# A gated MLP in seven products: a staged tile's place, and when four raw weight rows are loaded

## The chip, the cores and the metric

The kernel runs on one core of one Trainium2 chip. The metric is device time in microseconds (us) of one execution; the times shown are medians of a few runs. The profile is of one execution, taken by the hardware profiler.

## What is computed

```
g = x @ w_gate          # x: 2048 x 1024, w_gate and w_up: 1024 x 3584, bfloat16
u = x @ w_up
h = gelu(g) * u         # tanh approximation
out = h @ w_down        # w_down: 3584 x 1024
```

## The kernel before

The 2048 rows are worked on in two passes (`ip`) of two blocks (`c`) of 512 rows. A pass has a gate/up stage and a down stage. Both are written as Strassen-like schemes with seven block products instead of eight: sums and differences of blocks of the weights (`s1` to `s4`, `sums_s`, line 170), of x (`t1` to `t4`, line 155) and of the down weights are formed beside the products, and TensorE (PE) multiplies them as 128x128 weights against 128x512 blocks into eight PSUM banks.

**Gate/up stage.** It goes through 14 units of 256 columns, `u` = 0 to 13. Units 4 to 11 go in pairs (`pair0` in the first pass, line 357, `pair1` in the second), the others one by one (`unit`, line 238). For each unit the raw weights are loaded by two DMAs of 512 KB into a tile "w" (`load_w`, line 138), GpSimd (POOL) forms their sums (`pool`, line 110), ScalarE (ACT) copies banks to SBUF (`snap`, line 123) and applies the gelu (line 198), VectorE (DVE) adds and multiplies (`dve`, line 107; `times`, line 205, writes gelu(g)*u to h).

**Tiles and slots.** Three pools matter. `kpool` has 36 slots of 2 KB a partition, taken in turn by `slot` (line 97): gelu results, bank copies, raw rows and many others. A new tile takes a slot when its last tile's readers are done. `wpool` has three large buffers named "w": unit weights, later four raw rows of w_down together, and loads of made sums. `mpool` has two, named "m", for the sums of w_down.

**h that has no room yet.** While x's sums (`forms`) hold the place of the late part of h (`hL`), units 9 to 11 of the first pass put nine tiles elsewhere (`away`): eight in one "w" buffer (`staged`, line 296), the ninth in a slot of `kpool` named hx (line 865). `bring_home` (line 346) copies both to hL by DMA near the end of the last pair.

**The sums of w_down.** The down stage needs, for j = 0 to 13, three differences of blocks of w_down's rows. They are made once, in the first pass, and stored in DRAM (`td`, `store_made`, line 534). `fetch_wd` (line 501) loads the two raw rows of a j, 256 KB each: for j up to 9 into two slots, for 10 and 11, and for 12 and 13, four rows into one "w" buffer. Sums 0 to 9 are made by ScalarE and VectorE through a bank (`keep_part`, line 512, two of them in each pair, 8 in unit 12, 9 in unit 13), sums 10 to 13 by GpSimd alone (`keep_whole`, line 526, three subtractions each): 10 and 11 in `prepare` of unit 12, 12 and 13 in that of unit 13 (line 899). `making` (line 799) gives [8] for unit 12 and [9, 10, 11, 12, 13] for unit 13.

**Down stage** (`down`, line 630). Its steps are counted; an agenda says what is issued at a step (`at`, line 605), and `more` (line 964) adds stores and the next pass's loads. Steps 0 to 27 multiply h with raw tiles of w_down of 256 KB (`fetch12`, line 587, fourteen of them, numbered 0 to 13 here, each for two steps or eight matmuls; "tiles of the down stage"); the first four are fetched in unit 13 (line 935). Meanwhile `make12` (line 559) forms two sums of h for each j on VectorE, 28 operations whose operands lie in SBUF, and `load12` (line 541) loads the made sums back, at first two j's in a 1 MB DMA into a "w" buffer. From step 28 on come the products with those sums.

**What sets the order.** VectorE, GpSimd, PE and the DMA queue run in the order of the code (`ORDER`, line 69); ScalarE too in the gate/up stages. All DMAs are issued by SyncE (SP) on one queue, in order: an issue that waits holds up all behind it. In the built program an issue also waits until the DMA eight before it has landed.

Of the kernel before, what the change touches and what calls it, by code (L numbers as in the profile page):

```python
# [10 lines left out]
def kernel(  # L11
# [26 lines left out]
    P = nc.NUM_PARTITIONS  # L38
# [186 lines left out]
    def add(ps, other):  # L225
        g = new(dve, ps[0], other[0], ADD, "sum", dtype=f32)
        dve(ps[1], ps[1], other[1], ADD)
        return g, ps[1]

    def finish_raw(u, c, p1):  # L230
        g, up = add(c, p1)
        times(2 * u, 0, gelu(g), up)

    def into(ps, src):
# [3 lines left out]
    def unit(u, banks, s, t, late, after_p5, aside, keep, ahead_of_p4, behind_p4, turned):  # L238
        GU = range(2)
        e, c, d = banks  # L240
        aside(-2)
        g, up = late() if late else (None, None)
        aside(-1)
        for i in GU:
            product(e[i], s["s2"][i], t["t2"], False)
        aside(0)
        keep(0, c)
        u2 = [snap(e[i], "u2") for i in GU]
        if late:
            g = gelu(g)  # L250
        c11 = g, up
        keep(1, c)
        keep(2, c)
        c = d
        for i in GU:
            product(c[i], s["s1"][i], t["t1"], True)
        p5 = [snap(c[i], "p5") for i in GU]
        after_p5()
        for i in GU:
            product(e[i], s["s3"][i], t["t3"], False)  # L260
        if turned and u % 2:
            turned(banks[1])
        elif turned:
            g, up = add(e, p5)
            times(2 * u + 1, 1, gelu(g), up)
            turned(banks[1])
        else:
            g, up = new(dve, e[0], p5[0], ADD, "sum", dtype=f32), banks[1][not late]
            dve(up, e[1], p5[1], ADD)
        if late:  # L270
            times(2 * u, 0, *c11)
        for i in GU:
            product(c[i], s["s4"][i], t["tb"], False)
        if not turned:
            times(2 * u + 1, 1, gelu(g), up)
        aside(1)
        g, up = add(c, u2)
        times(2 * u, 1, gelu(g), up)
        if turned and u % 2:
            g, up = add(e, p5)  # L280
            times(2 * u + 1, 1, gelu(g), up)
        ahead_of_p4()
        for i in GU:
            product(e[i], s["sa"][i], t["t4"], False)
        behind_p4()
        if turned:
            dve(e[1], e[1], p5[1], SUB)
        times(2 * u + 1, 0, gelu(e[0]), e[1])
# [3 lines left out]
    T1, T2, T3, T4, TB = [[forms[:, 2 * n + i] for i in range(2)] for n in range(5)]  # L292
    pd = dpool.tile([P, LAST - FIRST + 1, 2, N], f32, name="pd")
    st8 = []

    def staged(n, c):
        if not st8:
# [513 lines left out]

    def raw_of(u, e):
        p1 = raw_products(e, K, xT, W(u))
        return lambda: finish_raw(u, K, p1)

    def upgraded(u):
        return FIRST <= u <= LAST
# [29 lines left out]
    for ip in range(NPASS):  # L847
        with tc.manual_schedule(engines={ENG.Activation}):
            if ip == 0:
                ws = {1: w, 2: ahead}  # L850
                late = lambda: add(cc, nxt["p1"])
            else:
                raw_of(0, F)()
                raw_of(1, C)()
            for u in range(1 if ip == 0 else 0, NU):
                if upgraded(u):
                    if u % 2:
                        continue
                    if u == FIRST:
                        S = {u: s, u + 1: sums_s(W(u + 1), pool)}  # L860
                    if (ip, u) == (0, FIRST):
                        for n in range(4):
                            for c in range(2):
                                away[NH + n, c] = lambda n=n, c=c: staged(n, c)
                        away[NH + 4, 0] = lambda: slot([P, N], bf16, "hx")

                    def hooks(what, n):
                        if what == "w":
                            W(n)
                            if ip == 0 and n - 3 in JS:  # L870
                                fetch_wd(JS[n - 3][1:])
                            if ip and n <= LAST:
                                fetch_p5(n)
                        if what == "home" and n == LAST:
                            bring_home()
                        if what == "pd":
                            k = 0 if n % 2 else KH
                            nc.sync.dma_start(
                                out=pd[:, n - FIRST].rearrange("p i n -> p (i n)"),
                                in_=flat(xT[1][:, k : k + KH]),  # L880
                            )
                        if what == "made":
                            store_made(n)
                        if what == "fetch":
                            fetch_wd(JS.get(n + 2, [8, 10, 11])[: 1 if n + 2 in JS else 3])

                    roles = F, C, K, E
                    if ip == 0:
                        F, C, K, E = pair0(u, roles, S, t, JS[u], hooks)
                    else:  # L890
                        F, C, K, E = pair1(u, roles, S, t, hooks)
                    if u + 1 == LAST:
                        s = make_s(None, pool, S[u + 2])
                        nxt["s"] = S[u + 3]
                    continue
                js = making(u) if ip == 0 else []
                first = (ip, u) == (0, 1)

                def prepare():
                    if first:  # L900
                        pool_behind(t["t4"][-1])
                    if u + 1 < NU:
                        nxt["s"] = make_s(W(u + 1), pool, nxt.get("s"))
                    if ip == 0:
                        if js:
                            store_made(js[0])
                        if u == NU - 2:
                            for j in making(u + 1)[1:3]:
                                keep_whole(j)
                        if u == NU - 1:  # L910
                            for j in js[3:]:
                                keep_whole(j)
                        if u == FIRST - 2:
                            fetch_wd(JS[FIRST][:1])

                def keep(part, ps):
                    if js:
                        keep_part(js[0], part, ps[part // 2])
                    if ip == 0 and u in (2, 3):
                        lo_part(u - 2, part, ps)  # L920

                def aside(part):
                    if first and part < 0:
                        rest_of_0(part + 2)
                    if part == 0 and u + 2 < NU:
                        W(u + 2)
                        if ip and upgraded(u + 2):
                            fetch_p5(u + 2)
                        if (ip, u) == (0, 1):
                            load_lo()  # L930
                    if part == 0 and (ip, u) == (0, NU - 2):
                        fetch_wd([9, 12, 13])
                    if part == 0 and (ip, u) == (0, NU - 1):
                        for n in range(4):
                            fetch12(n)
                            ahead12.add(n)
                        for j in js[1:3]:
                            store_made(j)
                    if part == 0 and "t4" not in t:
                        t.make("t4")  # L940

                def ahead_of_p4():
                    if u % 2 and u + 1 < NU:
                        raw_of(u + 1, F)()
                        nxt["c11"] = raw_of(u + 2, C)

                def behind_p4():
                    if "c11" in nxt:
                        nxt.pop("c11")()

                if u % 2 and not first:
                    E, K, C = C, E, K
                banks = (E, K, C) if u % 2 else (F, K, E)
                turned = (lambda c: lo_part(u - 2, 3, c)) if ip == 0 and u in (2, 3) else None
                unit(
                    u, banks, s, t, late if first else None, prepare, aside, keep,
                    ahead_of_p4, behind_p4, turned,
                )
                s = nxt.pop("s", None)
# [4 lines left out]
        def more(step):  # L964
            if last:
                return
            if step in (0, 2):
                store_made({0: NJ - 2, 2: NJ - 1}[step])
            if step == 0:
                xT[:] = new_x()  # L970
            if step >= 24 and step % 2 == 0 and step // 2 - 12 < len(moves):
# [43 lines left out]
```

## Time and profile before

| | us |
|---|---|
| median of 3 runs (540.96 to 541.69) | 541.0 |
| the profiled execution | 542.6 |
| its span, first to last instruction | 540.8 |
| PE busy | 531.4 |
| VectorE, ScalarE, GpSimd busy | 363.4, 276.2, 269.0 |
| DMA: hardware queue q1 | 103.44 MB, 64.4% of 16 engines |
| HBM read, written | 78.64 MB, 19.40 MB |
| first pass: gate/up ends, first 28 steps of down end | 200.1, 224.8 |
| second pass: gate/up begins, the down stage's products with w,q begin | 288.7, 473.8 |

The granted PE clock is 1.00 in the whole profile. In a timeline line come the start and the length in us, engine, source line, operation, out<-in by the program's names, the shape, how often it is repeated, and in brackets the idle time ahead of it and what ended that. Busy time of PE is counted with overlap: each matmul is some 0.38 us long and starts 0.22 us after the one before, so gaps are read from the starts. A line number is often that of a helper: L108 is any VectorE operation, L111 any of GpSimd's, L132 any matmul; the names of the tiles tell which.

### The profile page before, as it was taken

The page shows a single profiled execution, that of the slowest core. Times are in us where ns is not written, and L with a number is a line of the kernel's source. Part 1 is how long each engine was busy: PE and PEld are TensorE (multiplying, and loading weights), DVE is VectorE, ACT ScalarE, POOL GpSimd, SP SyncE. Part 2 cuts the span into 40 slices and gives each one's busy share as a digit, 9 for nine tenths or more (in the row PEclk, how much of TensorE's full clock was granted, in tenths as well). Part 3 has the DMA queues.
Part 4 walks back from the last instruction along what each step waited for, and adds up shares of the span by engine and source line. Part 5 has one row for each costly group of instructions (what it writes and reads, how often), then busy time and mean ns, then how long its engine had stood idle before and what let it go on. Part 6 is the DMA issues. An engine that isn't in the chain of part 4 may idle for free.

```text
span 540.8 us, 7482 instructions
## 1 busy us (share of the span) xinstructions
PE 531.4 (98%) x2372; PEld 377.5 (70%) x2393; DVE 363.4 (67%) x564; ACT 276.2 (51%) x497; POOL 269.0 (50%) x253
## 2 busy tenths in 40 slices
PE   9999999999999999999999999999999999999997
PEld 5568686868686664588886867668667685488886
DVE  2987867777775879658587455576675749775830
ACT  3557676868683741015345645656666551104351
POOL 1079986979798480000006949793979620000000
PEclk9999999999999999999999999999999999999999
DMA  9795063946769799989995443343561239655571
GB/s 245 174 232 167 1 175 117 279 150 196 233 196 320 252 388 365 337 253 216 259 322 151 122 137 99 115 120 113 160 189 28 57 102 383 235 175 161 170 240 53
DMA packets 115527, 103.91 MB, mean 192 GB/s; under 512 B 21792, under 2 KB 97696, under 8 KB 115360
## 3 DMA queue, kind: packets, MB, share of 16 engines
q1 hardware_dynamic: 115488, 103.44, 64.4%
q8 instruction: 19, 0.31, 0.3%
q14 instruction: 20, 0.16, 0.1%
HBM read 78.64 MB, written 19.40 MB: 181 GB/s over the span
## 4 chain that ended last, share of the span: by engine, by line
PE 89%; DMA 4%; DVE 3%; ACT 2%; issue 1%; SPq 0%; DVEq 0%; ACTq 0%
PE bank L132 89%; DMA raw<-in_w_down_dram 2%; DMA hL<-hx 1%; DVE bank L108 1%; DMA xn<-in_x_dram 1%; ACT g L200 1%; DVE hT L108 1%; DVE forms L108 0%; DVE sum L108 0%; DVE m L108 0%; DVE hL L108 0%; ACT bank L519 0%; SPq L707 0%; ACT forms L840 0%; ACT u L125 0%
## 5 line engine op out<-in xcount | busy, mean ns | idle before, releaser
L111 POOL TENSOR_TENSOR s<-w 128x512 fp32r<-128x512 bf16 x102 | 120.2, 1194 | 138.7 <-PE bank L132 107.5
L132 PE MATMUL bank<-t,s 128*128 128x512 f32 x552 | 132.1, 392 | 1.0 <-DVE m L108 0.7
L132 PEld LDWEIGHTS bank<-t,s 128*128 128x128 f32 x552 | 103.5, 188 | 23.9 <-DVE m L108 1.1
L132 PE MATMUL bank<-xT,w 128*128 128x512 bf16 (+1 forms) x489 | 108.0, 376 | 2.3 <-DMA raw<-in_w_down_dram 0.9
L132 PEld LDWEIGHTS <-w 128*128 128x128 bf16 x504 | 47.8, 98 | 60.0 <-issue 6.6
L200 ACT ACTIVATE g<-sum 128x512 f32<-128x512 f32 x81 | 51.5, 635 | 65.9 <-DVE sum L108 60.0
L125 ACT COPY p<-bank 128x512 f32<-128x512 f32 x102 | 57.7, 590 | 50.0 <-PE bank L132 50.0
L108 DVE TENSOR_TENSOR sum<-bank,p 128x512 f32<-128x512 f32 x54 | 37.1, 687 | 38.1 <-PE bank L132 37.0
L108 DVE TENSOR_TENSOR hT<-g,bank 128x512 bf16<-128x512 f32 x72 | 49.1, 687 | 16.3 <-ACT g L200 9.9
L111 POOL TENSOR_TENSOR s<-w,s 128x512 fp32r<-128x512 bf16 x50 | 57.9, 1174 | 0.9 <-PE bank L132 0.6
L111 POOL TENSOR_TENSOR s<-s,w 128x512 fp32r<-128x512 f32 x50 | 57.4, 1164 | 0.4
L132 PE MATMUL bank<-tb,s 128*128 128x512 f32 x216 | 54.4, 394 | 1.2 <-ACT p L125 1.2
L132 PE MATMUL bank<-t,sa 128*128 128x512 f32 x216 | 55.1, 397 | 0.0
L120 ACT CAST tb<-raw 128x512 fp32r<-128x512 bf16 x28 | 17.5, 630 | 73.4 <-PE bank L132 30.3
L108 DVE TENSOR_TENSOR bank<-bank,p 128x512 f32<-128x512 f32 x72 | 49.8, 695 | 7.4 <-PE bank L132 7.4
L132 PE MATMUL bank<-q 128*128 128x512 f32 x208 | 51.7, 389 | 0.0
L132 PEld LDWEIGHTS bank<-tb,s 128*128 128x128 f32 x216 | 40.4, 188 | 10.5 <-POOL w L111 1.5
L132 PEld LDWEIGHTS bank<-t,sa 128*128 128x128 f32 x216 | 40.6, 188 | 9.1
L132 PEld LDWEIGHTS bank<-q 128*128 128x128 f32 x208 | 39.0, 188 | 8.1
L125 ACT COPY u<-bank 128x512 f32<-128x512 f32 x56 | 32.1, 594 | 15.7 <-PE bank L132 15.7
L132 PE MATMUL bank<-raw,hT 128*128 128x512 bf16 x140 | 31.2, 379 | 0.2
L108 DVE TENSOR_TENSOR q<-raw 128x512 fp32r<-128x512 bf16 x28 | 19.2, 687 | 17.9 <-DMA raw<-in_w_down_dram 10.3
(80 smaller groups left out, 636.1 us busy)
## 6 DMA issues: line engine op xcount, KB each, us to landing
raw<-in_w_down_dram SPq DMA_DIRECT2D x72, 256.0 KB, 5.1
w<-in_w_gate_dram SPq DMA_DIRECT2D x27, 512.0 KB, 4.7
w<-in_w_up_dram SPq DMA_DIRECT2D x27, 512.0 KB, 5.9
q<-td SPq DMA_DIRECT2D x52, 256.0 KB, 4.4
td<-m SPq DMA_DIRECT2D x12, 768.0 KB, 5.3
w<-td SPq DMA_DIRECT2D x6, 1024.0 KB, 9.8
pd<-xT SPq DMA_DIRECT2D x8, 512.0 KB, 4.6
out_dram<-st SPq DMA_DIRECT2D x32, 128.0 KB, 1.9
```

The costliest lines, as they stand in the source:

```text
L108: nc.vector.tensor_tensor(out=out, in0=a, in1=b, op=op)
L111: nc.gpsimd.tensor_tensor(out=out, in0=a, in1=b, op=op)
L120: nc.scalar.copy(out=t, in_=src)
L125: nc.scalar.copy(out=t, in_=ps)
L132: nc.tensor.matmul(ps, lhsT=lhs, rhs=rhs, start=start, stop=stop, skip_group_check=True)
L200: nc.scalar.activation(g, src, ACT.Gelu_apprx_tanh)
```

## The change

Three edits, all in the first pass.

1. hx gets a tile of its own in the pool of x, and takes no slot.
2. The raw rows of j = 10 and 11 were loaded with those of 8 at the end of the last pair, and 12 and 13 with 9 in unit 12. Now 8 alone is loaded at the end of the last pair, 9, 10 and 11 in unit 12, and 12 and 13 in unit 13, after the first four tiles of the down stage and after the store of sum 10. The stores of sums 11, 12 and 13 are issued at steps 0, 3 and 6 of the down stage; before, 11 was stored in unit 13, and 12 and 13 at steps 0 and 2.
3. In unit 3, `times(2 * u + 1, 1, g, up)` moves on VectorE from ahead of `raw_of(u + 1, F)()` to between its adds and its own `times`. On ScalarE the gelu stays where it was.

The orders on PE, ScalarE and GpSimd are the same before and after; on VectorE one instruction moves by two places, on SP the loads and stores named above move.

```diff
-    def finish_raw(u, c, p1):
+    def finish_raw(u, c, p1, mid):
         g, up = add(c, p1)
+        if mid:
+            mid()
         times(2 * u, 0, gelu(g), up)
...
+        mid = None
         if turned and u % 2:
             g, up = add(e, p5)
-            times(2 * u + 1, 1, gelu(g), up)
-        ahead_of_p4()
+            g = gelu(g)
+            mid = lambda: times(2 * u + 1, 1, g, up)
+        ahead_of_p4(mid)
...
+    hx = xpool.tile([P, N], bf16, name="hx")
...
-                        away[NH + 4, 0] = lambda: slot([P, N], bf16, "hx")
+                        away[NH + 4, 0] = lambda: hx
...
                         if what == "fetch":
-                            fetch_wd(JS.get(n + 2, [8, 10, 11])[: 1 if n + 2 in JS else 3])
+                            fetch_wd(JS.get(n + 2, making(LAST + 1))[:1])
...
                     if part == 0 and (ip, u) == (0, NU - 2):
-                        fetch_wd([9, 12, 13])
+                        fetch_wd([9, 10, 11])
                     if part == 0 and (ip, u) == (0, NU - 1):
                         for n in range(4):
                             fetch12(n)
                             ahead12.add(n)
-                        for j in js[1:3]:
-                            store_made(j)
+                        store_made(js[1])
+                        fetch_wd(js[3:])
...
-                def ahead_of_p4():
+                def ahead_of_p4(mid):
                     if u % 2 and u + 1 < NU:
-                        raw_of(u + 1, F)()
+                        raw_of(u + 1, F)(mid)
...
-            if step in (0, 2):
-                store_made({0: NJ - 2, 2: NJ - 1}[step])
+            if step in (0, 3, 6):
+                store_made(NJ - 3 + step // 3)
```

More of the change, by code (lines that the diff above doesn't have):

```diff
@@ L813, in raw_of @@
         p1 = raw_products(e, K, xT, W(u))
-        return lambda: finish_raw(u, K, p1)
+        return lambda mid=None: finish_raw(u, K, p1, mid)
     def upgraded(u):
```

## The prediction

> **What bounds the kernel now.** I read the page first, then TensorE's timeline by stages, then what released the first instruction after each of its gaps, and at last the DMA queue. The profiled execution took 542.6 us, its span 540.8; the median of the runs shown is 541.0, so I work with differences and add them to the median.
>
> Page, parts 1 and 4: TensorE is busy for 98% of the span and holds 89% of the chain.
>
> ```profile
> PE 531.4 (98%) x2372; PEld 377.5 (70%) x2393; DVE 363.4 (67%) x564; ACT 276.2 (51%) x497; POOL 269.0 (50%) x253
> ...
> PE 89%; DMA 4%; DVE 3%; ACT 2%; issue 1%; SPq 0%; DVEq 0%; ACTq 0%
> ```
>
> A change off TensorE is worth only what it does to TensorE's gaps. Between 63 us and the end of the first pass's gate/up work they stand here (timeline of TensorE):
>
> ```profile
> 176.00 3.02 PE L132 MATMUL bank<-xT,w 128*128 128x512 bf16 x12 [0.93 <-DMA raw<-in_w_down_dram]
> ...
> 181.59 2.10 PE L132 MATMUL bank<-t,s 128*128 128x512 f32 x8 [0.71 <-DVE m L108]
> 183.94 2.06 PE L132 MATMUL bank<-t,s 128*128 128x512 f32 x8 [0.25 <-ACT u L125]
> ...
> 196.43 2.07 PE L132 MATMUL bank<-tb,s 128*128 128x512 f32 x8 [1.16 <-ACT p L125]
> ...
> 221.26 1.89 PE L132 MATMUL bank<-raw,hL 128*128 128x512 bf16 x7 [0.21 <-DMA raw<-in_w_down_dram]
> 223.31 1.89 PE L132 MATMUL bank<-raw,hL 128*128 128x512 bf16 x8 [0.16 <-DMA raw<-in_w_down_dram]
> ```
>
> The brackets count from the modelled end of the matmul before. From start to start, less the usual 0.22 us of one matmul, the six cost 1.1, 0.9, 0.4, 1.3, 0.4 and 0.3 us. The first is put down to a DMA that had long landed; ScalarE's timeline and the DMA issues' tell what it was:
>
> ```profile
> 174.59 0.63 ACT L200 ACTIVATE g<-sum 128x512 f32<-128x512 f32 x1 [4.63 <-DMA hL<-hx]
> ```
>
> ```profile
> 167.70 0.60 SPq L350 DMA_DIRECT2D hL<-hx  x1
> ```
>
> That gelu's result takes the slot in which hx lies, so it waits for hx's copy, which lands at 174.51.
>
> **hx gets its own place.** The gelu's sum ends at 171.28, so it starts 3.2 us earlier. Down the chain (times, kept sums of 7: lines 200, 108, 519) TensorE itself becomes the limit: ScalarE's second p1 copy must wait for four matmuls that end at 176.0 and can start 2.7 us earlier, not 3.2. The last kept sum of pair 7 (180.84 + 0.69 = 181.53) then ends near 178.75, 2.8 earlier; TensorE reaches the bank at 179.4, so the 0.9 gap goes too. I call the end of this sum X. The store of sum 7, pair 9, four big rows, the store of sum 8 and the first four tiles of the down stage hang on X in both orders in the same sequence, so the 1.3 gap at 196.43 (a kept sum waits for the store of sum 8) stays, X + 14.9. TensorE enters the down stage 2.8 us earlier. Bounds: 0 and 3.2; I take 2.8.
>
> **Order in unit 3.** VectorE's `times` of unit 3 moves behind two adds. Its timeline:
>
> ```profile
> 60.59 0.69 DVE L108 TENSOR_TENSOR hT<-g,bank 128x512 bf16<-128x512 f32 x1
> 61.19 0.68 DVE L108 TENSOR_TENSOR sum<-bank,p 128x512 f32<-128x512 f32 x1
> 61.80 0.69 DVE L108 TENSOR_TENSOR bank<-bank,p 128x512 f32<-128x512 f32 x1
> 62.59 0.69 DVE L108 TENSOR_TENSOR hT<-g,bank 128x512 bf16<-128x512 f32 x1
> ```
>
> The sum needs ScalarE's copy, which ends at 61.04. It can start at 61.1 instead of 61.19, the add at 61.7, the moved `times` at 62.3, and the one that TensorE waits for at 62.9 instead of 62.59 (starts are 0.60 apart). TensorE had 0.4 us of gap there and gets 0.3 more. Bounds -0.1 and +0.7 (a whole operation); I take **+0.3**. The shift carries on to X: 2.8 - 0.3 = 2.5.
>
> **The raw weights.** Before, rows 10 and 11 (four DMAs of 256 KB, 1.05 MB) load from 174.25 to 179.65, when the queue has nothing else; 12 and 13 follow in unit 12. After, 10 and 11 take the place of 12 and 13, and those come in unit 13 behind the down stage's first four tiles. Where it is then needed, the queue is full (windows: engines' busy in each stretch, clock, DMA share, GB/s):
>
> ```profile
> 182.00:198.00 16.00, 14.60 (x63) 11.26 (x62) 11.07 (x18) 11.15 (x21) 11.97 (x11) 1.00 1.01 367
> 198.00:208.00 10.00, 9.95 (x47) 5.19 (x47) 9.46 (x14) 1.16 (x3) 3.49 (x3) 1.00 1.02 345
> 208.00:224.00 16.00, 15.52 (x71) 6.92 (x72) 12.58 (x20) 2.05 (x4) 0.00 (x0) 1.00 1.04 389
> ```
>
> The mean over the 42 us is 370 GB/s. 1.05 MB more ahead of the down stage's tiles costs 2.8 us there, and the queue starts only 2.5 us earlier. The last of these tiles, which TensorE waits for, landed at 223.26 and would land at 223.6. So TensorE comes early to the down stage and waits for tiles: of the 2.5 us **nothing stays**, the sum up to here is +0.3.
>
> The Trainium skill, "DMA: Bandwidth & Descriptors", section "Where 436 GB/s comes from", has about 358 GB/s from HBM for one core; the windows show up to 389 in this stage. By 358 the extra bytes would be an estimated 2.9 us, which changes nothing.
>
> **GpSimd's sums are late, and meet VectorE.** GpSimd makes sums 10 to 13, three subtractions of 1.2 us each. Before, the twelve run from 185.98 to 202.19. After, rows 12 land behind the store of sum 10, X + 17.6 = 196.7, so the last six start at 196.7 and alone would end near 204. But VectorE starts `make12`, 28 operations on SBUF alone, 2.5 us earlier, at 198.8. Before, the two only touch, and the trace shows what a touch costs (VectorE, then GpSimd at that time and at 287):
>
> ```profile
> 201.29 1.45 DVE L108 TENSOR_TENSOR q<-hT 128x512 fp32r<-128x512 bf16 x1
> ```
>
> ```profile
> 199.79 2.40 POOL L111 TENSOR_TENSOR m<-w,m 128x512 fp32r<-128x512 bf16 x2
> ```
>
> ```profile
> 287.10 4.97 POOL L111 TENSOR_TENSOR s<-w 128x512 fp32r<-128x512 bf16 x2 [84.91 <-PE bank L132]
> ```
>
> VectorE's first took 1.45 us instead of 0.69: it ended 0.55 after GpSimd was done at 202.19. At 287.10 GpSimd's pair took 4.97 instead of 2.3, while VectorE ran such operations up to 289.94. They exclude each other. `make12` goes in pairs whose second waits for the first, with a hole of 0.1 us; I let GpSimd in at each hole, so that four subtractions meet it and the cycle is 2 x 0.6 + 1.15 = 2.3 us instead of 1.17. From 199.7: sum 12 ends at 200.9, sum 13 at 200.9 + 3 x 2.3 = 207.8, 3.6 us late. (Lower bound 204, no collision; upper: shut out until `make12` ends near 220.)
>
> The Trainium skill, "SBUF — State Buffer", section "SBUF: two separate sides", calls the pair of ports that VectorE and GpSimd share an exclusive lock, held for a whole instruction, which a VectorE operation with two SBUF inputs takes against a GpSimd one that reads SBUF. The two rows agree. It speaks against this change.
>
> Who waits: SP issues in order. The store of sum 12 stands ahead of tiles 6 and 7, and the first load of made sums (1 MB) waits for the last subtraction; behind it stand the store of sum 13 and tiles 8 to 13. Tile 8 was issued at 205.20, and is now issued near 209.3. All that went before has landed by 207, and a transfer's first bytes come some 1.8 us after its issue (a store of 0.79 MB alone: 4.26 us from issue to landing, less 2.1 at 370 GB/s, is 2.1). The queue is empty for about 2.8 us. The last tile: 223.6 + 2.8 = 226.4; if spacing behind tile 8 stays as before (11.4 us), 227.0. I take 226.6, 3.3 us late. With the tile's eight matmuls behind it, TensorE starts the next product 3.3 us later than at 224.84. From there TensorE is busy for 51.2 of 51.2 us up to 276 and for 173.5 of 174 up to 450, with the same order after the change; nothing is won back.
>
> Sum: +0.3 (unit 3) - 2.8 (hx) + 2.8 (bytes) + 3.0 (empty queue and spacing, 226.6 less 223.6) = **+3.3 us**: 544.3 against the median, 545.9 for the profiled execution.
>
> **Rivals.**
> A, the forecast, chance 0.55: 542.5 to 547.
> B, 0.22: GpSimd and VectorE interleave without loss (for: GpSimd's starts might win both holes; against: 287.10). Then +0.3: **541.3**, no change that a measurement of this kernel could tell, which is about 0.2%, 1.1 us.
> C, faster, 0.18: the queue is not what binds. In its best 2 us (194 to 196) it moved 422 GB/s; at that rate throughout, the 15.5 MB from the store of sum 7 to the last tile and the 0.7 that were moved ahead of it, from 179.8 on, are through at 218.2, TensorE never waits, and keeps 2.5 plus the 0.7 at 221 and 223: **537.8**; half of it, 539.4. It decides if the last tile lands before 222.1. Against it: 42 us at 370.
> D, 0.05: GpSimd is shut out until `make12` ends; over 548.
> That hx still holds up a gelu (the change doesn't do what it says) is in A and B: then X doesn't move, and the times are 2 us worse; I give it little, as the built program's gelu waits for its sum alone.
>
> Chances: faster 0.2 (C and a little of B), same 0.2, slower 0.6. Range 539.5 to 547: half of C and all of D lie outside.
>
> **What would show it.** Right: no wait for hL<-hx on ScalarE; no gap of TensorE at 174 to 182; the down stage begins near 197.6; 3 GpSimd subtractions on m and w at 198 to 208 with over 1.5 us each or holes between; SP silent from 202 to 207; TensorE gaps of 4 us near 211 and 2 us near 219 that wait for raw; 0.6 us gap at 63. Wrong: GpSimd's last m before 205; or the DMA share under 1 around 190 to 200, which would give C its chance.

## The result, and the profile after

| | before | after |
|---|---|---|
| median of 6 runs each, us | 541.35 (540.95 to 542.28) | 544.69 (543.79 to 546.38) |
| ratio | | 1.0062, interval 1.0043 to 1.0081 |
| the profiled execution, its span, us | 542.6, 540.8 | 543.79, 542.0 |

The changed kernel is slower by 0.6%, 3.3 us; the forecast was +3.3. The pair of profiles is only 1.2 us apart: the profiled execution of the changed kernel is the fastest of its six, that of the kernel before slower than all its timed runs. So sizes are read from the timed runs, and places from the profiles.

Page of the changed kernel, parts 1 and 4:

```profile
PE 532.5 (98%) x2372; PEld 378.9 (70%) x2393; DVE 366.4 (68%) x564; ACT 276.3 (51%) x497; POOL 270.3 (50%) x253
...
PE 88%; DMA 4%; DVE 4%; ACT 2%; issue 1%; SPq 1%; DVEq 0%; ACTq 0%
```

Still bound by TensorE; only its gaps have moved. Its timeline (start, length, engine, line, operation, in brackets the idle time ahead and what ended it):

```profile
174.24 3.63 PE L132 MATMUL bank<-xT,w 128*128 128x512 bf16 x16
...
193.05 2.08 PE L132 MATMUL bank<-tb,s 128*128 128x512 f32 x8 [0.54 <-ACT p L125]
...
213.91 2.66 PE L132 MATMUL bank<-raw,hT 128*128 128x512 bf16 x8 [3.14 <-DMA raw<-in_w_down_dram]
216.36 9.75 PE L132 MATMUL bank<-raw,hL 128*128 128x512 bf16 x39
225.77 6.50 PE L132 MATMUL bank<-w,q 128*128 128x512 f32 x27
```

The three gaps from 176 to 184 are gone, the one at 196 is now at 193 and smaller (how much of it there is varies from run to run, see hx_alone), and the two short waits at 221 and 223 have given way to one: 3.3 us in which TensorE has no work, in front of tile 8. ScalarE's gelu now waits for its sum alone:

```profile
171.52 0.63 ACT L200 ACTIVATE g<-sum 128x512 f32<-128x512 f32 x1 [1.36 <-DVE sum L108]
```

VectorE in unit 3, and TensorE behind it:

```profile
61.01 0.69 DVE L108 TENSOR_TENSOR sum<-bank,p 128x512 f32<-128x512 f32 x1 [0.56 <-ACT p L125]
...
62.22 1.27 DVE L108 TENSOR_TENSOR hT<-g,bank 128x512 bf16<-128x512 f32 x2
```

```profile
63.54 1.02 PE L132 MATMUL bank<-xT,w 128*128 128x512 bf16 x4 [0.50 <-DVE hT L108]
```

The moved `times` is the first of the x2, and TensorE waits for the second. From the start of the matmul ahead to the start of the one that waits it was 0.62 us and is now 0.88 (0.22 is the usual spacing of two matmuls; "start to start" below is counted in this way).

The windows (for each stretch the busy time of PE, PEld, VectorE, ScalarE and GpSimd, the granted clock of TensorE, the DMA share, GB/s):

```profile
198.00:208.00 10.00, 9.96 (x47) 4.47 (x46) 9.62 (x10) 0.00 (x0) 6.37 (x5) 1.00 0.92 303
208.00:224.00 16.00, 12.79 (x50) 5.42 (x51) 12.23 (x19) 2.05 (x4) 0.00 (x0) 0.89 1.04 382
```

The first row fell from 345 GB/s at share 1.02 to 303 at 0.92: the queue ran dry. The second has a clock of 0.89 where it was 1.00. What emptied the queue stands in SP's issues (SPq; `td<-w` and `td<-m` are stores of made sums, `w<-td` is a load of them, `raw` are tiles of the down stage) and on GpSimd (POOL):

```profile
199.94 0.33 SPq L540 DMA_DIRECT2D td<-w  x1
200.35 1.37 SPq L595 DMA_DIRECT2D raw<-in_w_down_dram  x2
204.63 0.37 SPq L550 DMA_DIRECT2D w<-td  x1
205.05 0.46 SPq L540 DMA_DIRECT2D td<-m  x1
205.60 1.51 SPq L595 DMA_DIRECT2D raw<-in_w_down_dram  x2
```

```profile
195.94 3.97 POOL L111 TENSOR_TENSOR w<-w 128x512 fp32r<-128x512 bf16 x3 [3.45 <-DMA w<-in_w_down_dram]
199.87 1.59 POOL L111 TENSOR_TENSOR m<-w 128x512 fp32r<-128x512 bf16 x1
201.54 3.06 POOL L111 TENSOR_TENSOR m<-w,m 128x512 fp32r<-128x512 bf16 x2
```

GpSimd waits 3.45 us for rows 12 and ends sum 13 at 204.60. SP issues nothing from 201.7 to 204.63: the next in its order is the first load of made sums (1 MB), and GpSimd's last subtraction, ending at 204.60, is what releases it. Behind it come the store of sum 13, and only then tile 8 (205.60).

### The profile page after: what moved, and what is told of

Same layout as the page of the kernel before. It is cut to its first block, busy times and chain, and to the rows that moved or that the text cites. A ratio compares the mean times of both kernels' runs of the same rounds, so it can differ in the third digit from the quotient of the medians.

```text
span 542.0 us, 7482 instructions
## 1 busy us (share of the span) xinstructions
PE 532.5 (98%) x2372; PEld 378.9 (70%) x2393; DVE 366.4 (68%) x564; ACT 276.3 (51%) x497; POOL 270.3 (50%) x253
## 4 chain that ended last, share of the span: by engine, by line
PE 88%; DMA 4%; DVE 4%; ACT 2%; issue 1%; SPq 1%; DVEq 0%; ACTq 0%
PE bank L132 87%; DMA raw<-in_w_down_dram 3%; DMA w<-in_w_up_dram 1%; DVE bank L108 1%; DVE s L108 1%; PE bank L774 1%; DVE hT L108 1%; ACT bank L524 1%; PE bank L719 1%; DVE forms L108 0%; DVE st L108 0%; ACT p L125 0%; ACT g L200 0%; DVE sum L108 0%; ACT forms L845 0%
```

## The experiments

Theory: three terms that add up, hx (a gain), the bytes ahead of the tiles (a loss), and SP standing in front of a DMA that waits for GpSimd (a loss). Rivals: the bytes alone; the collision of GpSimd and VectorE alone; the half clock behind TensorE's wait. Ratios are to the kernel before on the same chip, whose medians were 542.27, 542.15 and 542.07 us in the three groups of four runs; intervals are of 95%. The changed kernel's ratio is 1.0062, to a median of 541.35 us, so runs of different groups are better compared by ratios than by us.

| run | us | ratio | interval |
|---|---|---|---|
| hx_alone | 539.1 | 0.9944 | 0.9930 to 0.9958 |
| order_alone | 542.4 | 1.0002 | 0.9992 to 1.0012 |
| raw_alone | 547.4 | 1.0096 | 1.0080 to 1.0112 |
| hx_and_raw | 544.36 | 1.0048 | 1.0031 to 1.0065 |
| make12_behind | 543.74 | 1.0027 | 1.0009 to 1.0045 |
| tiles_ahead | 539.12 | 0.9940 | 0.9917 to 0.9962 |
| keep_busy | 544.84 | 1.0046 | 1.0028 to 1.0064 |
| hx_rows_early | 541.8 | 0.9983 | 0.9966 to 1.0000 |
| sums_early | 542.08 | 1.0004 | 0.9993 to 1.0016 |
| loads_behind | 540.42 | 0.9971 | 0.9960 to 0.9982 |
| stores_behind | 547.78 | 1.0113 | 1.0086 to 1.0139 |
| hx_best | 538.19 | 0.9930 | 0.9918 to 0.9942 |

### The parts one by one

**hx_alone**, the kernel before with this:

```diff
+    hx = xpool.tile([P, N], bf16, name="hx")
-    away[NH + 4, 0] = lambda: slot([P, N], bf16, "hx")
+    away[NH + 4, 0] = lambda: hx
```

> Before, with the one edit that hx lies in a tile of its own. Theory 1 (mine): the wait of the gelu for hx's copy holds TensorE up, and the queue behind it starts with the end of the kept sum of pair 7; with no bytes added and rows 10 and 11 still loaded in the idle time at 174, everything from there moves 2.8 us forward and stays there: about 538.5 us, ratio 0.995, and the gap of 1.3 us at the kept sum of unit 13 stays. Rival 1: the down stage's tiles are bound by the queue whatever comes before; then TensorE waits for them and the time stays at 541.3.

As expected, but for the gap ahead of the kept sum of unit 13, which did not stay at 1.3 us: it is 0.7 here. It is about as small in order_alone (0.7), where hx lies as before, and 1.2 and 1.3 in hx_and_raw and stores_behind, which have the new place of hx; so it varies from run to run, and its size can't be put down to hx. TensorE's timeline has a single gap left before the down stage, and no wait for a tile in front of tile 8:

```profile
193.31 2.07 PE L132 MATMUL bank<-tb,s 128*128 128x512 f32 x8 [0.57 <-POOL w L111]
...
197.03 15.71 PE L132 MATMUL bank<-raw,hT 128*128 128x512 bf16 x70
...
221.43 8.54 PE L132 MATMUL bank<-w,q 128*128 128x512 f32 x36
```

**order_alone**, the kernel before with the edit in unit 3 alone:

```diff
-    times(2 * u + 1, 1, gelu(g), up)
-    ahead_of_p4()
+    g = gelu(g)
+    mid = lambda: times(2 * u + 1, 1, g, up)
+    ahead_of_p4(mid)
```

> Before, with the order in unit 3 of the changed kernel alone. Theory 1: VectorE's times ends 0.3 us later, TensorE's gap at 63 us grows from 0.4 to 0.7 us, and 0.3 us stay: 541.6. Rival 1: the add that now comes first lets TensorE go earlier, 541.0 or less.

The gap grew from 0.62 to 0.89 us, the 0.3 of the forecast; the time cannot tell it from nothing.

**raw_alone**, the edit of the raw rows and the stores, with hx still in its slot:

```diff
-    fetch_wd([9, 12, 13])
+    fetch_wd([9, 10, 11])
...
-    for j in js[1:3]:
-        store_made(j)
+    store_made(js[1])
+    fetch_wd(js[3:])
```

> Before, with the new places of the raw loads and stores alone; hx stays in its slot. Theory 1: the parts add up, changed = hx (-2.8) + order (+0.3) + raw (+5.8), so here 545 to 547.5 us, TensorE waiting for raw tile 8 of the down stage. Rival 1: the new loads only take what hx's place frees (a wait behind a wait), then 542 to 543.5.

**hx_and_raw**, the changed kernel without the edit in unit 3:

```diff
-    g = gelu(g)
-    mid = lambda: times(2 * u + 1, 1, g, up)
-    ahead_of_p4(mid)
+    times(2 * u + 1, 1, gelu(g), up)
+    ahead_of_p4()
```

> The changed kernel with unit 3's order put back. Theory 1: 0.3 us less than the changed kernel, 544.4, with its gap at tile 8 and GpSimd's sums 12 and 13 in turn with VectorE. Rival 1: the order in unit 3 is what costs, then 541.5 or less.

Both as expected: -0.0056 and +0.0096 give +0.0040, beside +0.0048 measured for the two together. The whole loss is in the raw rows and stores. TensorE's timeline in hx_and_raw shows the same wait as the changed kernel, but longer:

```profile
215.20 3.57 PE L132 MATMUL bank<-raw,hT 128*128 128x512 bf16 x8 [4.43 <-DMA raw<-in_w_down_dram]
...
227.85 4.44 PE L132 MATMUL bank<-w,q 128*128 128x512 f32 x18
```

Tile 8 was issued at 205.49 here and at 205.60 in the changed kernel, and landed at 215.16 and 213.87. The wait has the same place in the queue and differs in length; the next product starts 3.0 us after that of the kernel before here, 0.9 us in the profile of the changed kernel.

### Bytes or waiting: splitting the loss

**sums_early** takes GpSimd's lateness away and leaves every DMA in its place (its sums 12 and 13 are not those of the reference):

```diff
         ra, rb = wraw[j]
+        if j >= NJ - 2:
+            ra, rb = [xT[0][:, 2 * i : 2 * i + 2].rearrange("p a n -> p (a n)") for i in range(2)]
...
+        if j == NJ - 1:
+            nc.gpsimd.tensor_copy(out=seen, in_=wraw[j][1][:, :2].bitcast(f32))
```

> The changed kernel, in which GpSimd makes sums 12 and 13 from columns of xT instead of rows 12 and 13, so that it need not wait for them (these two sums, and so the output, are not the reference's; one small GpSimd copy still reads row 13). Every DMA is as in the changed kernel, with the same bytes and the same place in SP's queue; only GpSimd's last six subtractions come earlier: they end near 200.5 instead of 204.6, and SP issues tile 8 near 201.5 instead of 205.6. The sum of the prediction (bytes 2.8, empty queue 3.0, apart from each other): 3.0 less than the changed kernel, 541.7. Rival 1 (the late subtractions are the whole loss, the bytes cost nothing): 5.2 less, 539.5. Rival 2 (the late subtractions are covered, the bytes are the whole loss): as the changed kernel, 544.7.

542.08, where the sum of the prediction asked for 541.7 and the rivals for 539.5 and 544.7. Against the changed kernel the late subtractions are 1.0062 - 1.0004 = 0.0058, 3.1 us; against hx_alone the moved rows are 1.0004 - 0.9944 = 0.0060, 3.2 us, of which 0.3 is unit 3. GpSimd is done at 200.2, and TensorE waits in several places, less in each (start to start 1.9, 0.85, 0.8 and 0.5 us):

```profile
212.47 1.89 PE L132 MATMUL bank<-raw,hT 128*128 128x512 bf16 x8 [1.50 <-DMA raw<-in_w_down_dram]
...
216.55 3.61 PE L132 MATMUL bank<-raw,hL 128*128 128x512 bf16 x16 [0.47 <-DMA raw<-in_w_down_dram]
```

**make12_behind** takes away the collision alone:

```diff
+    if step == -1:
+        nc.vector.tensor_copy(out=seen, in_=made[NJ - 1][:, 2, :1].bitcast(f32))
```

> The changed kernel, with one small VectorE copy that reads the third row of sum 13 ahead of make12, so that VectorE's 28 operations start only when GpSimd has made its last sum: the two no longer meet. Collision theory: GpSimd's last six subtractions run at 1.17 us each instead of 1.6 and end near 203.2 instead of 204.6; the first load of made sums and tile 8, which stand behind them in SP's queue, are issued 1.4 us earlier, TensorE's wait for tile 8 (3.3 us in the profile of the changed kernel) shrinks to about 2, and the time is 1.4 to 3 us below the changed kernel: 541.5 to 543.3. Rival (only the bytes in the queue bind, or tile 8 waits for what was issued ahead of it rather than for GpSimd): the same as the changed kernel, 544.5 within 0.8. If VectorE's later start makes q late for the product behind the first down pass, there is a wait for q at 225 and the time is above the changed kernel.

GpSimd's six ran at 1.2 us each and ended at 203.59, though they began 0.4 us later. The time is 0.95 us below the changed kernel by the medians, 1.9 by the ratios: above what the collision theory asked for, at the lower edge of the rival's range, and the intervals overlap a little. The trace does not tell where it was won: tile 8 was issued 1.0 us earlier than in the changed kernel (204.59) and landed 1.2 us later (215.03). As an estimate the collision is some 1 to 2 of the 3.1 us, and these runs do not fix it better; the rest would be that the rows come late, with or without it.

**tiles_ahead** moves what stands in front of the tiles:

```diff
-    AT12 = [6, 6, 10, 10, 14, 14, 16, 18, 20, 22, 27, 29, 31, 33]
+    AT12 = [18, 18, 18, 18, 19, 19, 19, 20, 21, 22, 27, 29, 31, 33]
...
-            if step in (0, 3, 6):
-                store_made(NJ - 3 + step // 3)
+            if step in (0, 12, 13):
+                store_made({0: NJ - 3, 12: NJ - 2, 13: NJ - 1}[step])
```

> The changed kernel, with the stores of sums 12 and 13 moved from steps 3 and 6 to steps 12 and 13 of the down stage and the first four loads of made sums behind them, so that SP issues tiles 6 to 11 without standing behind an instruction that waits for GpSimd. The bytes are the same. Theory of the in-order queue: tile 8 is issued before 203 instead of at 205.6, the wait of 3.3 us for it goes, and TensorE keeps what it saved upstream: 538 to 539.5. Rival (bytes bind): tiles 8 to 13 come no earlier than the queue can move what was put ahead, and with the made sums later by as much; TensorE waits for a later tile or for q's made sums, and the time stays at 541 to 544.5.

All of the loss is gone, with GpSimd as late as before (sum 13 ends at 204.57) and the same bytes. SP's issues and TensorE:

```profile
195.28 5.58 SPq L595 DMA_DIRECT2D raw<-in_w_down_dram  x6
200.96 0.42 SPq L540 DMA_DIRECT2D td<-w  x1
204.60 0.34 SPq L540 DMA_DIRECT2D td<-m  x1
205.03 2.37 SPq L595 DMA_DIRECT2D raw<-in_w_down_dram  x3
```

```profile
196.84 15.71 PE L132 MATMUL bank<-raw,hT 128*128 128x512 bf16 x72
...
220.83 8.54 PE L132 MATMUL bank<-w,q 128*128 128x512 f32 x36
```

SP still waits for GpSimd from 201.4 to 204.6, but tile 8 was issued ahead of it, and TensorE goes through without a gap. **loads_behind** and **stores_behind** do one half each.

```diff
-    AT12 = [6, 6, 10, 10, 14, 14, 16, 18, 20, 22, 27, 29, 31, 33]
+    AT12 = [18, 18, 18, 18, 19, 19, 19, 20, 21, 22, 27, 29, 31, 33]
```

> The changed kernel with the first loads of made sums behind tile 13 (as in the kernel with tiles ahead), but the stores of sums 12 and 13 left at steps 3 and 6 in front of tiles 6 and 8: SP still stands before them until GpSimd is done at 204.6, and the queue still runs empty for about a microsecond, but no load of 1 MB lies between that and tile 8. If it is the waiting in the queue that costs (the empty queue alone): tile 8 is issued at 205.1 as before, the time is near 544. If the loads' place ahead of the tiles makes the wait hurt (the first 1 MB took 5 us to land behind the empty queue): tile 8 lands by 209.8, behind the store of sum 13 alone, ahead of TensorE's need at 210.6, and the time is as with tiles ahead, 539.1.

```diff
-            if step in (0, 3, 6):
-                store_made(NJ - 3 + step // 3)
+            if step in (0, 12, 13):
+                store_made({0: NJ - 3, 12: NJ - 2, 13: NJ - 1}[step])
```

> The counterpart: the stores of sums 12 and 13 at steps 12 and 13, the loads of made sums at their places of the changed kernel, so that the first of them still waits for GpSimd's last subtraction and stands in front of tile 8. Tiles 6 and 7 come 4 us earlier, tile 8 is issued at 205.0 and lands at 211.5 behind the load, 1 us late instead of 3.3; the queue runs empty for longer, since nothing is there to be moved between 203 and 205. If the waiting is what costs, wherever it stands: 543 to 544.5. If it is the store of sum 13 and the bytes ahead of tile 8: 541 to 542.

With the loads behind, 540.42: SP waits just as long (tile 8 issued at 205.35), and yet tile 8 lands at 210.02 in its profile, the fastest of its runs, 0.9 us before TensorE is there (210.92). SP's issues:

```profile
204.92 0.34 SPq L540 DMA_DIRECT2D td<-m  x1
205.35 3.67 SPq L595 DMA_DIRECT2D raw<-in_w_down_dram  x6
```

That is near the second expectation, 1.3 us above it. So the late issue of tile 8 is not enough for the loss: three quarters of what tiles_ahead wins back (4.9 of 6.6 us by the ratios) come back when the loads of made sums alone no longer stand among the tiles. With the stores behind, 547.78, which neither expected. SP's issues:

```profile
209.70 0.41 SPq L595 DMA_DIRECT2D raw<-in_w_down_dram  x1
218.66 0.37 SPq L550 DMA_DIRECT2D w<-td  x1
```

```profile
221.10 2.66 PE L132 MATMUL bank<-raw,hL 128*128 128x512 bf16 x8 [2.44 <-DMA raw<-in_w_down_dram]
226.72 2.29 PE L132 MATMUL bank<-raw,hL 128*128 128x512 bf16 x5 [2.96 <-DMA raw<-in_w_down_dram]
```

The third load of made sums needs the "w" buffer in which sum 12 lies, and must wait until its store, now late, has landed at 218.60. The last two tiles are issued behind it, 9 us later. I had moved the store and forgotten whose buffer it frees.

### The half clock

In the changed kernel the matmuls from 215.08 to 218.07 start 0.427 us apart instead of 0.216 (a window of the changed kernel, the clock before the DMA share):

```profile
215.00:218.00 3.00, 3.00 (x8) 1.06 (x7) 2.93 (x6) 0.00 (x0) 0.00 (x0) 0.50 1.07 385
```

**keep_busy** fills the wait:

```diff
+    if not last and (kh, j) == (1, 2):
+        for _ in range(14):
+            matmul(c[0], zero, raw[1, 7][:, 0, :], False, False)
```

> The changed kernel, with 14 matmuls more between tiles 7 and 8 of the first down pass, with a weight tile of zeros, accumulated into a bank that is open there: they add zeros, so that the result is as before. They take 14 x 0.22 = 3.1 us and lie in TensorE's wait of 3.3 us for tile 8. Clock theory: TensorE's matmuls behind that wait, 0.427 us each for 3.3 us in the profile of the changed kernel, run at 0.22 again. What it is worth is disputed. Theory 1 (the last tile of this pass, landing at 224.0, sets the end in any case): at most 0.3 us, 544.0 to 544.8. Theory 2 (the slow stretch is part of the loss): 1.2 to 1.7 us less, 542.9 to 543.5.

```profile
210.59 3.19 PE L132 MATMUL bank<-raw,zero 128*128 128x512 bf16 x14
214.00 1.89 PE L132 MATMUL bank<-raw,hT 128*128 128x512 bf16 x8 [0.23 <-DMA raw<-in_w_down_dram]
...
224.15 1.89 PE L132 MATMUL bank<-raw,hL 128*128 128x512 bf16 x8 [0.16 <-DMA raw<-in_w_down_dram]
225.69 6.50 PE L132 MATMUL bank<-w,q 128*128 128x512 f32 x27
```

The clock is 1.00 throughout, and no gain can be told: 544.84, 0.9 us less than the changed kernel by the ratios, well within the intervals. TensorE is earlier at tiles 9 to 13 and waits there instead; the next product starts at 225.69, in the changed kernel at 225.77. With the clock kept up the last tile, which lands at 224.11, sets the end; in the changed kernel it lands at 224.04, and TensorE begins it at 224.23. So the half clock cost 0.1 to 0.2 us there.

### Can it be had better?

**hx_rows_early** is hx_alone with the store of sum 8 ahead of rows 12 and 13 in the queue, for the gap at 193:

```diff
                             store_made(js[0])
                         if u == NU - 2:
+                            fetch_wd([12, 13])
...
-                        fetch_wd([9, 12, 13])
+                        fetch_wd([9])
```

> The kernel before with hx in a tile of its own, and besides the load of rows 12 and 13 for GpSimd (four DMAs, 1.05 MB) put behind the store of sum 8 instead of ahead of it in SP's queue. The store is issued 2.9 us earlier and lands at about 185 to 187 instead of 190.7; the kept sum that reuses its tile then waits for nothing, and the last gap of TensorE between 63 us and the down stage (0.96 us from start to start at 192.3 in the kernel with hx alone) goes. If the chain of waits ends there: 0.7 less than hx alone, 538.3. Rival: the down stage is bound by the landing of its tiles, which are behind the same bytes as before; then what is won at 193 is lost in front of a tile, and it is the same as hx alone, 539.1.

The gap at 193 went, and the time rose above that of hx_alone; neither expectation had that. GpSimd and SP:

```profile
197.68 1.15 POOL L111 TENSOR_TENSOR m<-w 128x512 fp32r<-128x512 bf16 x1 [3.36 <-DMA td<-m]
```

```profile
194.76 0.64 SPq L591 DMA_DIRECT2D raw<-in_w_down_dram  x1
201.99 0.32 SPq L536 DMA_DIRECT2D td<-m  x1
202.40 1.39 SPq L591 DMA_DIRECT2D raw<-in_w_down_dram  x2
```

Sum 13's tile waits for the store of sum 10 to land; SP waits with sum 13's store at the head of the queue, and tiles 6 and 7 behind it are issued 2.9 us later than in hx_alone. It is the mechanism of the change once more, by another door. **hx_best** adds the order of tiles_ahead:

```diff
-            if step in (0, 2):
-                store_made({0: NJ - 2, 2: NJ - 1}[step])
+            if step in (12, 13):
+                store_made(step)
```

and the AT12 of tiles_ahead.

> The kernel with hx in a tile of its own and rows 12 and 13 behind the store of sum 8 (541.8), with the stores of sums 12 and 13 moved to steps 12 and 13 and the loads of made sums behind tile 13. If its loss against hx alone is again SP standing before a store that waits for GpSimd (there GpSimd's third m tile waits 3.4 us for the store of sum 10, and the store of sum 12 is issued at 202.0 instead of 199.1), the tiles now come in time, TensorE has neither the gap at 193 nor the waits from 206 to 223, and the time is 0.7 to 1.2 below hx alone: 538.0 to 538.4. If rows 12 and 13 delay the tiles by their bytes: 540 to 542.

(The store meant there is that of sum 13, not 12.) 538.19, as the first theory has it: 0.7% below the kernel before and the best of all, though its interval overlaps those of hx_alone and tiles_ahead. TensorE's timeline has no gap with a reason between 174 and 230.

## Why the prediction was right, and where it was not

- **hx, -2.8**: right. The kept sum that the chain hangs on ends at 178.77 (forecast 178.75; it was 181.53). hx_alone measured 3.2 us; in its profile 0.6 lies in the gap at 193, which the prediction kept at 1.3 us and which is 0.7 there; as order_alone has it as small, that part can't be put down to hx. hx_rows_early shows that this gap is the store of sum 8, as said.
- **Unit 3, +0.3**: right in the gap (0.26), too small to be seen in the time.
- **Bytes, +2.8**: right in size, by sums_early less hx_alone, 2.9. That it is bytes and nothing else is not shown: with tiles_ahead the same bytes cost nothing, since the loads of made sums, not the tiles, give way. It is the order in the queue that makes them cost.
- **The empty queue, +3.0**: right in size (3.1), and in the chain of late rows, SP held and tile 8 late. Its inner numbers were wrong, and that they made up for each other is luck. The step "the cycle is 2.3 us" was mis-sized: GpSimd got in behind every VectorE operation, not only at the hole of each pair, and its operations came 1.6 us apart, so that sum 13 ended at 204.60, not 207.8, and tile 8 was issued at 205.60, not 209.3. The stretch without transfers was shorter too. The rate of the changed kernel from 200 us on, in slices of 0.45 us:

```profile
GB/s 355 373 414 366 394 262 246 223 344 376 314 39 80 73 91 191 391 391 355 300 191 273 401 419 460 398 325 353 394 435 419 430 428 419 364 385 355 373 389 407
```

  Four slices are under 100 GB/s, 1.8 us, where the sum had 2.8 us empty. What the sum lacked is that the queue did not come back at its full rate at once. The windows of 2 us of the changed kernel:

```profile
204.00:206.00 2.00, 2.00 (x11) 0.89 (x10) 1.90 (x3) 0.00 (x0) 0.60 (x1) 1.00 0.80 196
206.00:208.00 2.00, 1.96 (x10) 0.87 (x9) 1.93 (x4) 0.00 (x0) 0.00 (x0) 1.00 0.76 236
208.00:210.00 2.00, 1.98 (x10) 0.92 (x10) 1.97 (x4) 1.57 (x4) 0.00 (x0) 1.00 1.01 296
```

  and of hx_alone:

```profile
204.00:206.00 2.00, 2.00 (x11) 0.93 (x10) 1.97 (x4) 0.00 (x0) 0.00 (x0) 1.00 1.05 403
206.00:208.00 2.00, 2.00 (x11) 0.88 (x9) 1.93 (x4) 0.00 (x0) 0.00 (x0) 1.00 1.03 394
208.00:210.00 2.00, 1.95 (x10) 0.89 (x10) 1.97 (x4) 1.32 (x3) 0.00 (x0) 1.00 1.08 399
```

  Instead of 2.39 MB in these 6 us it moved 1.46; the missing 0.93 MB are 2.3 us at hx_alone's rate. The first load of 1 MB landed 5.0 us after the transfer before it, in hx_alone 2.6. The lost time costs this much only because loads of made sums stand among the tiles: in loads_behind tile 8 is issued as late (205.35) and the queue moves 298 to 304 GB/s in the same three windows, and most of the loss is gone. (The sum also took 1.8 us from an issue to its first bytes where its own row gives 2.1; with 2.1 the term would have been 3.3.)
- **Where TensorE waits**: 4 us near 211 came as 3.3 (4.4 in hx_and_raw); the wait near 219 did not come. As keep_busy shows, the half clock lets TensorE reach the later tiles after they land, and hides their lateness.
- **Rivals**: B (no loss by the collision) fell, since the wait is there even without a collision. C had the wrong condition, since the queue does bind (sums_early waits for tiles with GpSimd in time), but its price, 537.8 to 539.4, is near what reordering earns (539.12, 538.19). Its 0.7 MB should be the 1.05 MB of the bytes term, which changes nothing in its price.
- "Wrong: GpSimd's last m before 205" was a bad sign to name: it came (204.60), and the loss came too.

## What to carry to other kernels

A queue that issues in order is held by its first waiting entry, and what stands right behind that entry goes ahead of all later ones when it is free again. When a load is moved later, ask which engine's result becomes late, where the store of that result stands in the queue, whose buffer the store frees, and which urgent tile is issued behind it. Put what must wait behind what must not: here a reorder alone was worth 5.6 us by the medians (544.7 to 539.1), 6.6 by the ratios, with the same bytes and the same late engine.

## What the runs showed of the hardware

- **VectorE and GpSimd took turns.** With two-input operations on SBUF from both, GpSimd's took 1.53 to 1.6 us (1.2 alone) and VectorE's 1.46 and 1.64 (0.69 alone); neither was shut out. Two of VectorE's in the changed kernel:

```profile
200.38 1.64 DVE L108 TENSOR_TENSOR q<-hT 128x512 fp32r<-128x512 bf16 x1
202.12 1.46 DVE L108 TENSOR_TENSOR q<-q,hT 128x512 fp32r<-128x512 f32 x1
```

  One of each took 1.6 us, less than the 1.9 of the two one after the other. The Trainium skill, "SBUF — State Buffer", section "SBUF: two separate sides", says that the one that comes second is blocked for the whole instruction; here some 0.3 us of each pair overlapped. Turns are not all that was seen: in the prediction's row at 287.10, the first of GpSimd's two took 3.86 us, and ended 1.0 us after the last of a row of VectorE operations that followed each other without a hole and kept their 0.68 us. What decides between the two was not tried.
- **A wait of some 3 us was followed by the half clock.** In the changed kernel the half rate (0.427 us a matmul) set in 1.2 us after the end of a wait of 3.3 us and held for 3.0; in hx_and_raw, after a wait of 4.6 us, it set in within 0.4 us and held for some 5. The Trainium skill, "TensorE: Matmul & The Clock Gate", section "Part 1: The HAM clock gate", gives about 3.4 us without work as what brings the half clock, and as long to leave it. The second is near the 3.0, and short of the 5. For the first, less was enough: in stores_behind a wait of 2.6 us, with one of 1.5 us shortly before it, was followed by the half rate, while the 1.7 us in sums_early was not.
- **A queue that ran dry came back slowly.** The first 1 MB load behind the gap in SP's issues landed 5.0 to 6.0 us after the transfer before it (changed kernel, hx_and_raw, make12_behind), against 2.6 in hx_alone and 3.7 in sums_early, where the queue was full. In make12_behind it was issued 1.0 us earlier than in the changed kernel, and landed 1.5 us later. Why is open; no run here tried it.
